# Re-cutting the loads at the start and at the end of a one-core cached-attention block: x and c in seven pieces for five, the last V tile in two for three, w2 in four for five, and two warm-up products for three

## The chip, the core and the metric

The kernel runs on one core of a Trainium2 chip. The core has a matrix engine (TensorE, PE in the profile; its weight loads are PEld), a vector engine (VectorE, DVE), a scalar engine (ScalarE, ACT), GpSimd (POOL) and a sequencer that does nothing but issue transfers (SyncE, SP). Sixteen DMA engines move data between the device memory and the core's on-chip memory. The metric is the device time of one execution in microseconds (us). The kernel before takes 393.93 us, the median of three runs that lie between 393.89 and 394.06 us.

## What is computed

Eight decode rows of a transformer block with conditioning: `x` and `c` are 8 x 512, there are 32 query heads on 8 key/value heads of size 128, and only the last 2048 of 8192 cached positions count. All numbers are float32.

```python
mod = (silu(c) @ w_mod)                       # 512 x 3072, cut into sa, ca, ga, sb, cb, gb
h = layernorm(x) * (1 + ca) + sa
q = (h @ wq)                                  # 512 x 4096
p = softmax(q k^T / sqrt(128))                # k, v: the last 2048 cached positions
x = x + ga * ((p v) @ wo)                     # 4096 x 512
h = layernorm(x) * (1 + cb) + sb
x = x + gb * (relu(h @ w1 + b1)**2 @ w2 + b2) # w1: 512 x 1792, w2: 1792 x 512
```

The keys and values that count are 8 x 8 x 2048 x 128 floats each, 134 MB of the 165 MB that one execution reads.

## The kernel before

One call of `tile_adaln_cached_attention_mlp` writes every engine's instructions out in a fixed order. There is no loop left at run time.

**The big loads.** The on-chip home of the streamed data is one tile `home` with four slots of 4 MB, and a tile `small` of 2 MB. The list `loads` (line 144) names what is streamed, in order: the two parts of `w_mod` (`mod 0`, 4 MB, and `mod 1`, 2 MB), `wq` (8 MB, two slots in one transfer), then the 16 K tiles and 16 V tiles of 4 MB with pieces of `wo` between them, and at the end the last of `wo`, two halves of `w1`, and `w2`. `pump` (line 152) issues the next load whenever the slot that it needs is free; all of these transfers are issued by SP, in this order. A few loads are cut into pieces, so that a consumer can begin with the first piece: the last V tile by `cuts` on line 103 (a half and two quarters), `w2` by the list on line 136 (row groups 0 to 8, 8 to 10, 10 to 12, 12, 13).

**The small loads.** `x` and `c` come as one array `xc`, in four groups of eight rows (line 65). Each group is one transfer of 8 rows x 256 floats or two of 8 rows x 128 floats (line 67); they are issued by ACT. The first of them waits until DVE has cleared the tile `xc_in`. Late in the kernel ACT also issues the loads of `b1` and `b2` (lines 503 and 504).

**Counters.** The program keeps eight counters of landed transfers, named DMAHW0 to DMAHW7, and the loads take them in turn, those of ACT and those of SP in one sequence. Before, `mod 0` has DMAHW0, the five pieces of `xc` have 1 to 5, `mod 1` has 6, `wq` has 7, and the first K tile has 0 again. A load that gets a counter for a second time is issued only when the load that had it before has landed: this is a wait of the issuing engine, and what stands behind it on that engine waits too.

**Compute.** At the start, `c` goes through silu (line 201 and on) and PE multiplies it with `w_mod` (L278), a normalised `x` becomes `h`, and PE multiplies it with `wq` (L304). For every K tile DVE transposes (L190), PE forms scores (L359), DVE and ACT make the softmax, and PE weighs V (L446). At the end come the products with `wo` (L486), then `w1` (L611), then the 56 products with `w2` (L630), which run through the 14 row groups of `w2` in order, two last steps on DVE (L638, L639), and the transfer of the result (L640). Ahead of the `w2` products stand three products of a constant whose result nobody reads, `spin(3)` on line 627 (L566); they keep PE at work while DVE makes the operand `rT`.

Of the kernel before, what the change touches and what calls it, by code (L numbers as in the profile page):

```python
# [19 lines left out]
def tile_adaln_cached_attention_mlp(  # L20
# [16 lines left out]
    B, HKV, SK, DH = k_cache.shape  # L37
# [26 lines left out]
    nc.vector.memset(xc_in, 0.0)  # L64
    for q in range(D // P):
        b = slice(32 * q, 32 * q + B)
        for x, y in ((0, 2),) if q < 3 else ((0, 1), (1, 2)):
            nc.scalar.dma_start(xc_in[b, x:y], xc[b, x:y])

    ident = consts.tile([P, P], F32, name="ident")  # L70
# [8 lines left out]
    big = NJ * DH  # L79
# [9 lines left out]
    def size_of(key):  # L89
        return "small" if key[0] in ("wo", "w1") or key == ("mod", 1) else "big"  # L90

    def load(key):
        kind, i = key
        held[key] = free[size_of(key)].pop(0)
        if key == ("wq", 0):
            return
        t = slots[size_of(key)][held[key]]
        if kind in "KV":

            hk, c = divmod(i, 2)  # L100
            v = k_cache[4 * c : 4 * c + 4, hk] if kind == "K" else v_cache[c::2, hk]
            v = v[:, SK - W :, :].rearrange("u (p j) d -> p u (j d)", j=NJ)
            cuts = (0, big // 2, big * 3 // 4, big) if key == ("V", 2 * HKV - 1) else (0, big)
            for x, y in zip(cuts, cuts[1:]):
                nc.sync.dma_start(t[:, x:y], v[..., x:y])
            return

        def rows(o, v):
            n = v.shape[1] * v.shape[2]
            nc.sync.dma_start(t[:, o : o + n].rearrange("p (a n) -> p a n", n=v.shape[2]), v)  # L110

        w1v = w1.rearrange("(p kc) n -> p kc n", p=P)

        def wo_rows(j):

            r = 2 * REP * DH
            return wo[j * r : (j + 1) * r, :].rearrange("(h p i) n -> p h (i n)", p=P, i=4)

        if kind == "wo":
            rows(0, wo_rows(i))  # L120
        elif kind == "mod":

            v = w_mod.rearrange("(p kc) n -> p (kc n)", p=P)
            nc.sync.dma_start(t, v[:, big:] if i else v[:, :big])
        elif kind == "wq":

            o = base[held["wq", 0]]
            nc.sync.dma_start(home[:, o : o + 2 * big], wq.rearrange("(p k) n -> p (k n)", p=P))
        elif kind == "tail":
            rows(0, wo_rows(HKV // 2 - 1))  # L130
            rows(big // 2, w1v[:, 0:2])
        elif kind == "w1":
            rows(0, w1v[:, 2:4])
        else:
            v = w2.rearrange("(p c) n -> p c n", p=P)
            for lo, hi in ((0, 8), (8, 10), (10, 12), (12, 13), (13, 14)):
                rows(D * lo, v[:, lo:hi])

    def slot(key, n, o=0):
# [12 lines left out]
    def pump():  # L152
        while at[0] < len(loads) and free[size_of(loads[at[0]])]:
            load(loads[at[0]])
            at[0] += 1
# [53 lines left out]
    lo = consts.tile([P, 1], F32, name="lo")  # L209
    hi = consts.tile([P, 1], F32, name="hi")  # L210
# [299 lines left out]
    for s in range(N + PV_LAG + 1):  # L510
        g, i = divmod(s, C)
        q, h = divmod(s, 2)
# [50 lines left out]
    def spin(n):  # L563

        for _ in range(n):
            nc.tensor.matmul(spin_ps, ident, ident[:, None, :].to_broadcast([P, 4, P]), start=True, stop=True)  # L566
# [57 lines left out]

    py = ps_m.tile([P, 512], F32, name="m_ps", tag="m_ps")
    nc.tensor.matmul(py[:, :P], qsel.rearrange("p q b -> p (q b)"), b2_in, start=True, stop=False)
    spin(3)
    for f in range(FC):
        for q in range(NQ):
            nc.tensor.matmul(  # L630
# [6 lines left out]
    y = work.tile([P, P], F32, name="y", tag="one_y", bufs=1)  # L637
# [39 lines left out]
```

## Time and profile before

| | |
|---|---|
| time, median of 3 runs | 393.93 us |
| time of the profiled execution | 394.02 us |
| its span, first to last instruction | 392.2 us |
| mean granted clock of PE | 0.891 |
| read from device memory | 164.67 MB, 420 GB/s over the span |
| PE, DVE, ACT busy (share of the span) | 65%, 56%, 12% |
| instructions | 4670 |

The span begins with the first instruction and ends with the last; about 1.8 us of the time lie outside it. A row of the page's table of instruction groups reads: line, engine, operation, what it writes and reads, how often, then busy time, mean length, and the idle time of the engine just before these instructions with what ended it. "SPq" and "ACTq" are the two engines that issue transfers. A row on a transfer gives the time from its issue until all of it has landed.

### The profile page before, as it was taken

To read this page: it belongs to the slowest core of one execution; us is meant where nothing else is said; L and a number is where in the kernel's file an instruction comes from. 1 tells how busy PE (TensorE), PEld (TensorE's weight loads), DVE (VectorE), ACT (ScalarE), POOL (GpSimd) and SP (SyncE) were. 2 spreads that over 40 slices of the span, in tenths; PEclk is the share of its full clock that TensorE was granted. 3 is DMA by queue.
4 is the path that set the end of the run, shared out by engine and by line. 5 is a ranking of instruction groups with operands and counts; after the bars stand their busy time and mean duration, and the time that the engine had idled before them with its cause. 6 is when DMAs were issued, how large, how long until landed. Compare 5 with 4: busy or idle time off the path is not lost.

```text
span 392.2 us, 4670 instructions
## 1 busy us (share of the span) xinstructions
PE 255.1 (65%) x2006; PEld 77.7 (20%) x2006; DVE 219.7 (56%) x315; ACT 46.3 (12%) x89; POOL 1.3 (0%) x8
## 2 busy tenths in 40 slices
PE   0091958879228973797384837873774828896796
PEld 0030211112002321222021202221221202233324
DVE  1261099889056835783582817780775457855222
ACT  0120011221003100310031003000201003004010
POOL 0000000000000000000000000000000000000000
PEclk9997789989859996999699688999796969998989
DMA  8999999999999999999999999999999999999994
GB/s 329 430 435 439 440 435 431 428 430 401 453 428 428 426 431 428 430 431 446 423 426 435 428 433 435 430 424 431 407 450 431 426 431 436 432 423 408 427 424 178
DMA packets 7685, 165.04 MB, mean 421 GB/s; under 512 B 832, under 2 KB 1008, under 8 KB 1520
## 3 DMA queue, kind: packets, MB, share of 16 engines
q1 hardware_dynamic: 7568, 164.70, 98.3%
q8 instruction: 16, 0.26, 0.3%
q10 hardware_dynamic: 96, 0.04, 0.0%
q14 instruction: 5, 0.04, 0.0%
HBM read 164.67 MB, written 0.07 MB: 420 GB/s over the span
## 4 chain that ended last, share of the span: by engine, by line
DMA 62%; PE 19%; DVE 16%; issue 2%; SPq 0%; ACT 0%; DVEq 0%; ACTq 0%
DMA home<-in_A_k_cache_dram 46%; DVE kT L190 12%; DMA home<-in_A_wq_dram 9%; PE s_ps L359 8%; DMA home<-in_A_wo_dram 7%; PE m_ps L304 3%; PE o_ps L446 2%; PE q_ps L566 1%; DVE pT L425 1%; PE wo_ps L486 1%; PE m_ps L630 1%; PE m_ps L611 1%; PE p_ps L390 1%; DVE qbd L322 1%; DVE pr L418 1%
## 5 line engine op out<-in xcount | busy, mean ns | idle before, releaser
L190 DVE STREAM_TRANSPOSE kT<-home 128x1024 f32<-128x1024 f32 x128 | 151.1, 1219 | 87.0 <-DMA home<-in_A_k_cache_dram 83.6
L359 PE MATMUL s_ps<-kT,qst 128*32 128x512 f32 x512 | 129.4, 1076 | 21.5 <-DVE kT L190 20.6
L446 PE MATMUL o_ps<-home,pT 128*32 128x256 f32 x1024 | 69.8, 396 | 11.1 <-DVE pT L425 9.6
L446 PEld LDWEIGHTS o_ps<-home,pT 128*32 128x32 f32 x1024 | 33.5, 116 | 101.2 <-issue 60.5
L375 PE MATMUL m_ps<-ident,mx 128*1 128x128 f32 x16 | 4.3, 364 | 59.8 <-DVE mx L373 59.8
L359 PEld LDWEIGHTS s_ps<-kT,qst 128*32 128x32 f32 x512 | 14.5, 116 | 41.5 <-DVE kT L190 33.2
L425 DVE STREAM_TRANSPOSE pT<-pr 128x2048 f32<-128x2048 f32 x8 | 18.2, 2272 | 1.0 <-ACT pr L408 1.0
L408 ACT ACTIVATE pr<-pr,own 128x512 f32<-128x512 f32 x16 | 17.9, 1233 | 0.3
L402 ACT ACTIVATE pr<-p_ps,nm 128x512 f32<-128x512 f32 x8 | 5.5, 688 | 97.1 <-DVE nm L399 97.1
L369 ACT COPY ss<-s_ps 128x512 f32<-128x512 f32 x8 | 4.7, 587 | 100.6 <-issue 72.4
L347 ACT COPY qst<-q_ps 32x128 f32<-32x128 f32 x32 | 8.2, 257 | 70.2 <-PE q_ps L336 69.9
L304 PE MATMUL m_ps<-home,h1T 128*32 128x512 f32 x64 | 10.0, 793 | 8.7 <-DMA home<-in_A_wq_dram 8.7
L375 PEld LDWEIGHTS m_ps<-ident,mx 128*1 128x1 f32 x16 | 0.7, 81 | 65.0 <-DVE mx L373 65.0
L224 PE MATMUL m_ps<-xsum,sel 128*128 128x1 f32 x2 | 0.6, 362 | 19.8 <-DVE xsum L222 19.8
L322 DVE COPY qbd<-m_ps 32x128 f32<-32x128 f32 x8 | 3.0, 372 | 18.1 <-PE m_ps L319 18.0
L390 PE MATMUL p_ps<-ss,perm 128*128 128x512 f32 x16 | 11.3, 794 | 0.0
L399 DVE TENSOR_SCALAR nm<-m_ps 128x1 f32<-128x1 f32 x8 | 1.3, 158 | 15.8 <-PE m_ps L395 15.8
L418 DVE TENSOR_SCALAR pr<-pr,own 128x512 f32<-128x512 f32 x16 | 9.2, 657 | 0.8 <-ACT pr L402 0.8
L202 DVE TENSOR_SCALAR e_sb<-e_sb 128x128 f32<-128x128 f32 x1 | 0.2, 226 | 14.4 <-ACT e_sb L201 14.4
L429 PE MATMUL m_ps<-zs,tsel 128*128 128x8 f32 x16 | 2.9, 252 | 8.1 <-DVE zs L420 8.1
L463 DVE TENSOR_SCALAR o_sb<-o_ps,bit 128x128 f32<-128x128 f32 x16 | 4.9, 304 | 4.9 <-PE o_ps L446 4.9
L373 DVE TENSOR_REDUCE mx<-s_ps 128x1 f32<-128x512 f32 x8 | 5.3, 662 | 3.8 <-ACT ss L369 3.8
(124 smaller groups left out, 125.8 us busy)
## 6 DMA issues: line engine op xcount, KB each, us to landing
home<-in_A_k_cache_dram SPq DMA_DIRECT2D x16, 4096.0 KB, 27.0
home<-in_A_v_cache_dram SPq DMA_DIRECT2D x15, 4096.0 KB, 20.0
small<-in_A_wo_dram SPq DMA_DIRECT2D x3, 2048.0 KB, 31.1
home<-in_w_mod_dram SPq DMA_DIRECT2D x1, 4096.0 KB, 12.5
small<-in_w_mod_dram SPq DMA_DIRECT2D x1, 2048.0 KB, 16.9
home<-in_A_v_cache_dram SPq DMA_DIRECT2D x1, 2048.0 KB
home<-in_A_v_cache_dram SPq DMA_DIRECT2D x2, 1024.0 KB, 21.2
home<-in_A_wo_dram SPq DMA_DIRECT2D x1, 2048.0 KB, 25.5
```

What stands on the lines that cost most here:

```text
L190: nc.vector.transpose(KTS[q, j][:, rows], k[:, rows, 32 * j : 32 * j + 32])
L304: nc.tensor.matmul(pqs[r][32 * g : 32 * g + 32, :], hT[:, kc, :], w[:, 4 * r + g, :], start=(kc == 0), stop=(kc == NQ - 1),)
L322: nc.vector.tensor_copy(qbd[b, 4 * r : 4 * r + 4, j].rearrange("p g (b t) -> p t g b", t=REP), pT_[b].rearrange("p (t g b) -> p t g b", t= ...
L347: nc.scalar.copy(own[b, :, :, i, 0], pq[b, :P].rearrange("p (c m t) -> p c m t", c=2, t=REP))
L359: nc.tensor.matmul(s_ps[0][32 * g : 32 * g + 32, :], qst[hk % 2][:, P * (4 * c + u) + 32 * j :][:, :32], kT[:, u], start=(c == 0 and j == ...
L373: nc.vector.tensor_reduce(mx, s_ps[0], axis=AX.X, op=ALU.max)
L390: nc.tensor.matmul(sp, perm, SS_.pop(hk), start=True, stop=True)
L402: nc.scalar.activation(pr.rearrange("p j x -> p (j x)"), SS_.pop(hk), AF.Exp, bias=nm, scale=SCALE, accum_out=z)
L408: nc.scalar.mul(X_[hk][..., w], pr, own[:, w : w + 1])
L418: nc.vector.tensor_scalar(X_[hk][..., w], pr, own[:, w : w + 1], None, op0=ALU.mult)
L425: nc.vector.transpose(PT_[hk].rearrange("p e j r -> p j e r"), X_.pop(hk).rearrange("p j x w -> p j (x w)"))
L446: nc.tensor.matmul(O_[n][32 * g : 32 * g + 32, : 2 * DH], PT_[hk][:, e, j : j + 2].rearrange("p j r -> p (j r)"), vt[:, j : j + 2, :].rear ...
```

## The change

The change has four parts. The groups of eight rows of `xc` were three single transfers and one pair, and are now one single transfer and three pairs. The last V tile is loaded in two halves. Row groups 8 to 12 of `w2` are one transfer of 1 MB where they were two of half a megabyte. One of the three products of `spin` ahead of the `w2` products is gone.

```diff
@@ -64,7 +64,7 @@
     for q in range(D // P):
         b = slice(32 * q, 32 * q + B)
-        for x, y in ((0, 2),) if q < 3 else ((0, 1), (1, 2)):
+        for x, y in ((0, 2),) if q < 1 else ((0, 1), (1, 2)):
             nc.scalar.dma_start(xc_in[b, x:y], xc[b, x:y])
@@ -100,7 +100,7 @@
-            cuts = (0, big // 2, big * 3 // 4, big) if key == ("V", 2 * HKV - 1) else (0, big)
+            cuts = (0, big // 2, big) if key == ("V", 2 * HKV - 1) else (0, big)
             for x, y in zip(cuts, cuts[1:]):
                 nc.sync.dma_start(t[:, x:y], v[..., x:y])
@@ -133,7 +133,7 @@
             v = w2.rearrange("(p c) n -> p c n", p=P)
-            for lo, hi in ((0, 8), (8, 10), (10, 12), (12, 13), (13, 14)):
+            for lo, hi in ((0, 8), (8, 12), (12, 13), (13, 14)):
                 rows(D * lo, v[:, lo:hi])
@@ -624,7 +624,7 @@
-    spin(3)
+    spin(2)
     for f in range(FC):
```

The first place is the start of the program on SP. The rows are the first seven loads, each with the counters and engines that it waits for; `home` and `small` are the on-chip tiles, and the two loads from `w_mod` are `mod 0` and `mod 1`. Before:

```order
L124 DMA home<-in_w_mod_dram 128x8192
L124 DMA small<-in_w_mod_dram 128x4096
L128 DMA home<-in_A_wq_dram 128x16384
L105 DMA home<-in_A_k_cache_dram 128x1x8192 [waits DMAHW0_49]
L105 DMA home<-in_A_k_cache_dram 128x1x8192 [waits DMAHW1_49,PE_49]
L105 DMA home<-in_A_k_cache_dram 128x1x8192 [waits DMAHW7_49,DMAHW2_49,PE_49]
L105 DMA home<-in_A_v_cache_dram 128x1x8192 [waits DMAHW3_49,PE_49]
```

The same seven loads in the changed kernel:

```order
L124 DMA home<-in_w_mod_dram 128x8192
L124 DMA small<-in_w_mod_dram 128x4096 [waits DMAHW0_49]
L128 DMA home<-in_A_wq_dram 128x16384 [waits DMAHW1_49]
L105 DMA home<-in_A_k_cache_dram 128x1x8192 [waits DMAHW2_49]
L105 DMA home<-in_A_k_cache_dram 128x1x8192 [waits DMAHW3_49,PE_49]
L105 DMA home<-in_A_k_cache_dram 128x1x8192 [waits DMAHW4_49,DMAHW1_49,PE_49]
L105 DMA home<-in_A_v_cache_dram 128x1x8192 [waits DMAHW5_49,PE_49]
```

The seven pieces of `xc` now hold counters 1 to 7, so `mod 1` gets DMAHW0, the counter of `mod 0`, and has a wait that it did not have; `wq` gets DMAHW1, that of the first piece of `xc`, and also has a wait that it did not have.

The second place is the end of the program on SP, as a piece of the difference between the two (rows with - stand only before, with + only now); `in_B_w_dram` stands for `w1` and `w2`, and the loads of `w2` are the four or five last ones ahead of the result.

```order
 L105 DMA home<-in_A_v_cache_dram 128x1x8192 x2
-L105 DMA home<-in_A_v_cache_dram 128x1x4096
-L105 DMA home<-in_A_v_cache_dram 128x1x2048 x2
+L105 DMA home<-in_A_v_cache_dram 128x1x4096 x2
 L110 DMA home<-in_A_wo_dram 128x2x2048
 L110 DMA home<-in_B_w_dram 128x3584
 L110 DMA small<-in_B_w_dram 128x3584
 L110 DMA home<-in_B_w_dram 128x4096
-L110 DMA home<-in_B_w_dram 128x1024 x2
+L110 DMA home<-in_B_w_dram 128x2048
 L110 DMA home<-in_B_w_dram 128x512 x2
 L640 DMA out_dram<-y 128x128
```

Two loads fewer are issued there; the order of the others is the same, and no other engine's order differs but PE's, by the one constant product, and ACT's, by the pieces of `xc`.

## The prediction

> **What bounds the kernel now.** I read the page first. Its second part shows the share of the sixteen DMA engines' time in 40 slices, and its fourth part the chain of waits that ended last.
>
> ```profile
> span 392.2 us, 4670 instructions
> DMA  8999999999999999999999999999999999999994
> DMA 62%; PE 19%; DVE 16%; issue 2%; SPq 0%; ACT 0%; DVEq 0%; ACTq 0%
> ```
>
> The engines are at 9 tenths or more in all slices but the first and the last, and the chain is mostly waits for loads. The DMA view cut to the stretch from 2.4 to 385.2 us says how full that is (queue, packets, MB, share of sixteen engines' time):
>
> ```profile
> DMA packets 7268, 163.93 MB, mean 428 GB/s; under 512 B 779, under 2 KB 827, under 8 KB 1117
> q1 hardware_dynamic: 7152, 163.61, 99.8%
> ```
>
> The queue that SP fills keeps all sixteen engines busy for 99.8% of those 382.8 us. There is no idle time in which a lost moment could be made good: a hole in the queue is paid in full at the end, and time on the other engines counts only where it makes the queue run dry, or behind the last load.
>
> Next I read the timeline of the first 16 us, where the counters of the loads are first used again (start, length, engine, line):
>
> ```profile
> 0.73 0.39 SPq L124 DMA_DIRECT2D home<-in_w_mod_dram  x1
> 1.16 2.03 ACTq L68 DMA_DIRECT2D xc_in<-in_xc_dram  x5
> 1.18 0.42 SPq L124 DMA_DIRECT2D small<-in_w_mod_dram  x1
> 1.64 0.42 SPq L128 DMA_DIRECT2D home<-in_A_wq_dram  x1
> 13.29 0.63 SPq L105 DMA_DIRECT2D home<-in_A_k_cache_dram  x1
> 15.10 1.28 ACT L201 ACT_TABLE_LOAD   x1 [15.10 <-DMA xc_in<-in_xc_dram]
> ```
>
> SP puts 14 MB into the queue within 2.1 us: `mod 0`, `mod 1`, `wq`. Its fourth load goes at 13.29. The view of SP's waits says why (who waited for whom, total, times, longest):
>
> ```profile
> SPq L105 <- DMA home<-in_w_mod_dram: 11.2, 1, 11.2
> ```
>
> That is the counter DMAHW0: the first K tile waits until `mod 0` has landed. It costs nothing there, since `mod 1` and `wq` are queued behind `mod 0` meanwhile.
>
> **The pieces of xc.** Seven pieces take seven counters, so that `mod 1` inherits the counter of `mod 0`. SP will then issue `mod 1` where it now issues the first K tile, at about 13.3 us and not at 1.18; `wq` stands behind it on SP and goes at 13.7, the first K tile after that. The queue holds nothing but `mod 0` until then, so the engines run dry, and the queue starts anew. How long a start lasts is bounded by the page's rows on issues (KB, us from issue to landing):
>
> ```profile
> home<-in_w_mod_dram SPq DMA_DIRECT2D x1, 4096.0 KB, 12.5
> small<-in_w_mod_dram SPq DMA_DIRECT2D x1, 2048.0 KB, 16.9
> out_dram<-y SPq DMA_DIRECT2D x1, 64.0 KB, 1.6
> ```
>
> `mod 1` lands now at 1.18 + 16.9 = 18.1 us. `mod 0` met an empty queue: 4.19 MB at 428 GB/s are 9.8 of its 12.5 us, and 2.7 are start and landing. The result's transfer also meets an empty queue: 0.07 MB are 0.15 of its 1.6 us, and 1.45 are start and landing. The 2.1 MB of `mod 1` flow in 4.9 us. With the one, `mod 1` would land at 13.3 + 2.7 + 4.9 = 20.9 us, 2.8 later than now; with the other at 13.3 + 1.45 + 4.9 = 19.65, 1.55 later. The row of `mod 0` is the nearer one: the same tensor, direction, 128 rows and size of pieces but for a factor of two. I take 2.4 and not its whole 2.8, because its 2.7 us hold things that are not paid again: the pieces of `xc` that share the engines with it, and the sixteen engines' first pieces at the program's start. That they are not instantaneous shows the DMA view of the first 3 us, in 40 slices of 0.075 us:
>
> ```profile
> GB/s 0 0 0 0 0 0 0 0 0 0 0 0 0 0 0 0 0 0 0 0 0 0 0 1748 1748 1311 0 0 437 0 0 437 437 437 0 437 0 0 0 0
> ```
>
> The first piece starts in the 24th slice, 1.0 us after the issue at 0.73, and the last engine's first one at 2.7. Both ends stay in the range.
>
> The Trainium skill, page "DMA: Bandwidth & Descriptors", section "Anatomy of one DMA — SWDGE (gpsimd) path", gives a fixed cost of about 2.0 us per transfer, for transfers issued by GpSimd; worked out from that page the landing would be at 13.3 + 2.0 + 4.9 = 20.2 us and the sum an estimated 396.0. The two rows of this trace, both of SP's transfers, lie on either side of that figure (1.45 and 2.7).
>
> The change of `xc` has another side, on ACT. Its five issues take 2.03 us, so that seven take about 2.8, and silu waits for the last piece, now until 15.10. A later or earlier arrival is covered by this row of the page's costliest groups:
>
> ```profile
> L304 PE MATMUL m_ps<-home,h1T 128*32 128x512 f32 x64 | 10.0, 793 | 8.7 <-DMA home<-in_A_wq_dram 8.7
> ```
>
> PE waits 8.7 us for `wq` after all work on `c` and `x` is done, and 2.4 us more when `wq` comes later. Two more pieces would have to add over 8 us; the five together landed in 15. I cost this at nothing. The same cover holds for the loads that wait for PE's use of `mod 0`.
>
> **The last V tile.** Its third quarter now lands together with the fourth. The DMA view of 345.0 to 345.7 us has the fourth quarter's landing, and the timeline the work behind it:
>
> ```profile
> 345.12 0.54 SPq L105 DMA_DIRECT2D home<-in_A_v_cache_dram  x1
> home<-in_A_v_cache_dram SPq DMA_DIRECT2D x1, 1024.0 KB, 21.2
> ```
>
> ```profile
> 366.05 1.90 PE L446 MATMUL o_ps<-home,pT 128*32 128x256 f32 x32
> 370.05 0.19 DVE L475 TENSOR_TENSOR oT<-tr,rz 128x32 f32<-128x32 f32 x1
> 371.34 0.16 PEld L486 LDWEIGHTS wo_ps<-home,oT 128*32 128x32 f32 x8 [2.23 <-DMA home<-in_A_wo_dram]
> ```
>
> The quarter lands at 345.12 + 21.2 = 366.3. The last 32 passes on PE, the work of half a tile, take 1.90 us and now begin at 366.05; they would begin at 366.3 and end 0.25 later. The operand `oT` is then ready at 370.5, and the product with `wo` waits for its own load until 371.34. The slack of 1.1 us covers the 0.25: nothing.
>
> **w2 and the constant product.** The timeline of the end, and the DMA view of the last piece of `w2`:
>
> ```profile
> 366.41 0.33 SPq L110 DMA_DIRECT2D home<-in_B_w_dram  x1
> home<-in_B_w_dram SPq DMA_DIRECT2D x1, 256.0 KB, 22.2
> ```
>
> ```profile
> 382.88 2.84 PE L566 MATMUL q_ps<-ident 128*128 128x512 f32 x6
> 383.98 0.28 DVE L623 SCALAR_TENSOR_TENSOR pr<-relu 128x112 f32<-128x112 f32 x1
> 385.65 2.78 PEld L630 LDWEIGHTS m_ps<-home,pr 128*32 128x32 f32 x104 [0.76 <-issue]
> 388.63 0.16 PEld L630 LDWEIGHTS m_ps<-home,pr 128*32 128x32 f32 x8 [0.21 <-DMA home<-in_B_w_dram]
> 389.77 0.35 SPq L640 DMA_DIRECT2D out_dram<-y  x1
> ```
>
> Each product is two passes, so the three constant ones are six in 2.84 us, and one is 0.95. Without it the `w2` products begin at 384.7, still behind `rT` (384.26). But the last piece lands at 366.41 + 22.2 = 388.6, and the last eight passes wait for it already, 0.21 us. Starting earlier makes that wait longer and the end no earlier: nothing. The merged piece has two of 256 KB behind it, 0.52 MB or 1.2 us, so it lands at about 387.4; 40 of the 104 passes (2.78 us, 27 ns each) need it or follow it before the last piece, 1.1 us, and end at 388.5, ahead of 388.6. So the merge adds nothing either.
>
> Two loads fewer on SP's queue save what a load costs a full queue. Of the 382.8 us 0.2% is not that queue's work, 0.8 us over some 46 loads, so at most 0.02 each. I take 0.05 for both.
>
> **The sum.** Against the profiled execution's 394.02 us: 394.02 + 2.4 - 0.05 = 396.4. The median of the runs lies 0.09 below that execution; the forecast for the median is 396.3 us.
>
> **The rivals.** The first is on the other side: *no hole*. The wait on `mod 0`'s counter is met before the engines run dry. It decides at the point where the counter is full more than 1.0 us (the first-piece delay above) ahead of the engines' last piece of `mod 0`. Then only the tail's edits are left, each worth nothing or 0.05: 393.9 us, no change. Against it: the first K tile waited for this very counter and went at 13.29, beside 0.73 + 12.5 = 13.2 for the full landing; what speaks for it is only that no view shows when the pieces end. 6 in 100, with 2 more for a gain over 0.2% that I can't see.
>
> The second is *a dearer start*: seven pieces and two new waits make a second hole, `wq` coming too late behind `mod 1`. Its condition is that 2.1 MB (4.9 us) drain before `wq`, issued 0.45 us later, begins to flow, which would need a delay of over 4 us where the rows show 1.0 to 2.7. With a second start of 1.45 us the time is 397.8.
>
> The third is *a colder PE at the end*. PE stands still for up to 0.8 us ahead of the merged piece; if the granted clock fell, the 48 last passes would take longer. Rows by stage (after the busy times: granted clock, DMA share, GB/s):
>
> ```profile
> 38.00:48.00 10.00, 9.54 (x64) 2.64 (x64) 0.00 (x0) 0.34 (x1) 0.00 (x0) 0.68 1.03 441
> 386.00:387.00 1.00, 1.00 (x47) 1.00 (x42) 0.00 (x0) 0.00 (x0) 0.00 (x0) 1.00 0.53 211
> ```
>
> The clock was 0.68 behind an 8.7 us wait and 1.00 at the end. 48 passes at 27 ns are 1.3 us, at 0.68 they are 1.9; less the 0.1 of slack it is 0.5 more, 396.8. The Trainium skill, "TensorE: Matmul & The Clock Gate", Part 1, has the clock fall after an idle window of about 3.4 us; by that rule this rival does not come about, and the trace agrees as far as it goes. With the second it gets 9 in 100 beyond the range's upper end.
>
> **How the numbers follow.** A hole of about 2.4 us: 80 in 100 within the range. Its low end is the low row, 393.93 + 1.55 - 0.05 = 395.4, less 0.4 for `mod 0` landing sooner with nothing queued behind it: 395.0. The high end is 393.93 + 2.8 + 0.25, if the V tile's cover fails: 397.0. A smaller hole (394.7 to 395.0) has 3 in 100. A measurement of this kernel tells about 0.2%, 0.8 us, from no change. Slower: 80 + 9 + 3 = 92 in 100; within 0.2%: 6; faster: 2.
>
> **What the changed profile would show.** SP's rows would have `mod 1` at about 13.3 and `wq` at 13.7; the time from issue to landing of `mod 1` would be about 7 us instead of 16.9; the DMA slices of the first 20 us would have a hole near 13 to 15; the wait of ACT for `xc` would be no longer than now; everything from `wq` on would stand 2 to 3 us later; at the end PE would still wait for the last piece of `w2`, longer than 0.21 us. I am wrong if SP issues `mod 1` early, if the queue's later stretches turn out to have idle time that takes the shift in, or if a restart moves bytes much sooner than either row.

## The result, and the profile after

The changed kernel takes 396.63 us (median of six runs, 396.33 to 396.69), the kernel before 394.06 us on the same chips (six runs, 393.89 to 394.35). The ratio is 1.0063, with a 95% interval from 1.0052 to 1.0074: slower by 2.6 us. A few executions take 3 to 4 us longer than the others of their kernel (398.2 to 398.3 of the kernel before, 400.0 and 401.3 of the kernel with `xc` alone), so medians are given, and where such an execution is among them the interval of a ratio is wide. The profiled execution of the changed kernel took 396.65 us, its span is 394.9 us, 2.7 more than before.

The page of the changed kernel, parts 2 and 4 (shares of the DMA engines in 40 slices; the chain that ended last by engine):

```profile
span 394.9 us, 4667 instructions
DMA  8899999999999999999999999999999999999994
DMA 59%; DVE 22%; PE 14%; issue 4%; ACT 0%; SPq 0%; DVEq 0%; ACTq 0%
```

One slice has changed, the second, which reaches from 9.9 to 19.7 us: 8 tenths where 9 stood. The chain is still mostly waits for loads. The timeline of the start of the changed kernel:

```profile
0.73 0.39 SPq L124 DMA_DIRECT2D home<-in_w_mod_dram  x1
1.16 2.69 ACTq L68 DMA_DIRECT2D xc_in<-in_xc_dram  x7
13.21 0.33 SPq L124 DMA_DIRECT2D small<-in_w_mod_dram  x1
13.59 0.42 SPq L128 DMA_DIRECT2D home<-in_A_wq_dram  x1
14.06 0.64 SPq L105 DMA_DIRECT2D home<-in_A_k_cache_dram  x1
14.09 1.28 ACT L201 ACT_TABLE_LOAD   x1 [14.09 <-DMA xc_in<-in_xc_dram]
```

`mod 1` goes at 13.21 and not at 1.18. SP's waits in the changed kernel name what it waited for (who for whom, total, times, longest), and the page's rows on issues give the time to landing:

```profile
SPq L124 <- DMA home<-in_w_mod_dram: 12.1, 1, 12.1
```

```profile
home<-in_w_mod_dram SPq DMA_DIRECT2D x1, 4096.0 KB, 12.5
small<-in_w_mod_dram SPq DMA_DIRECT2D x1, 2048.0 KB, 7.6
```

The hole itself is seen in the DMA view from 12 to 16 us, 40 slices of 0.1 us, GB/s by the time at which a piece of a transfer starts. Before, and then after:

```profile
GB/s 0 164 164 169 671 835 497 328 164 0 655 983 492 328 0 164 502 998 671 328 0 164 328 655 819 655 0 0 164 983 819 492 164 0 164 819 983 328 328 0
```

```profile
GB/s 0 0 10 57 21 26 36 16 0 0 0 0 0 0 0 0 0 0 0 0 0 328 164 655 164 819 164 164 164 0 0 0 0 328 819 328 328 492 0 328
```

Before, a new piece starts in most tenths of a microsecond (32 of 40). After, only small amounts (the pieces of `xc`) start up to 12.8, then nothing until 14.1, 0.9 us after SP's issue. The last piece of `mod 0` itself starts between 11.4 and 11.5 (the DMA view from 10 to 14 us), so SP's queue starts nothing for 2.6 us; the pieces begun before still flow for a part of that. `mod 1` lands at 13.21 + 7.6 = 20.8 us where it landed at 18.1: 2.7 us later, and the span is 2.7 us longer. Nothing in between takes any of it in, as the DMA view of the changed kernel from 16 to 388 us shows for SP's queue:

```profile
q1 hardware_dynamic: 6776, 159.45, 100.0%
```

The end of the changed kernel, in its timeline:

```profile
374.12 0.16 PEld L486 LDWEIGHTS wo_ps<-home,oT 128*32 128x32 f32 x8 [0.88 <-DMA home<-in_A_wo_dram]
374.16 0.19 DVE L475 TENSOR_TENSOR oT<-tr,rz 128x32 f32<-128x32 f32 x1
384.77 1.98 PE L566 MATMUL q_ps<-ident 128*128 128x512 f32 x4
387.72 1.95 PE L630 MATMUL m_ps<-home,pr 128*32 128x128 f32 x64 [0.97 <-DMA home<-in_B_w_dram]
390.06 1.03 PEld L630 LDWEIGHTS m_ps<-home,pr 128*32 128x32 f32 x40 [0.66 <-DMA home<-in_B_w_dram]
391.36 0.16 PEld L630 LDWEIGHTS m_ps<-home,pr 128*32 128x32 f32 x8 [0.26 <-DMA home<-in_B_w_dram]
392.49 0.35 SPq L640 DMA_DIRECT2D out_dram<-y  x1
```

PE now waits for the first, the merged and the last piece of `w2` (0.97, 0.66 and 0.26 us), and goes on with the last one at 391.36, 2.73 us after the 388.63 of before. The end still hangs on the landing of the last bytes.

### The profile page after: what moved, and what is told of

The parts are those of the page before. It is cut to its first block, busy times and chain, and to the rows that moved or that the text cites. A ratio compares the mean times of both kernels' runs of the same rounds, so it can differ in the third digit from the quotient of the medians.

```text
span 394.9 us, 4667 instructions
## 1 busy us (share of the span) xinstructions
PE 255.0 (65%) x2004; PEld 78.1 (20%) x2004; DVE 219.7 (56%) x315; ACT 46.2 (12%) x89; POOL 1.3 (0%) x8
## 4 chain that ended last, share of the span: by engine, by line
DMA 59%; DVE 22%; PE 14%; issue 4%; ACT 0%; SPq 0%; DVEq 0%; ACTq 0%
DMA home<-in_A_k_cache_dram 37%; DVE kT L190 13%; DMA home<-in_A_wq_dram 7%; DMA home<-in_B_w_dram 6%; DMA home<-in_A_v_cache_dram 6%; PE s_ps L359 5%; DVE pT L425 4%; DMA home<-in_w_mod_dram 3%; PE p_ps L390 3%; PE m_ps L304 3%; DVE pr L418 2%; PE o_ps L446 2%; DVE mx L373 1%; DVE qbd L322 1%; PE m_ps L375 1%
## 5 line engine op out<-in xcount | busy, mean ns | idle before, releaser
L446 PE MATMUL o_ps<-home,pT 128*32 128x256 f32 x1024 | 71.1, 401 | 10.9 <-DVE pT L425 9.7
L446 PEld LDWEIGHTS o_ps<-home,pT 128*32 128x32 f32 x1024 | 34.4, 118 | 102.1 <-issue 59.8
L202 DVE TENSOR_SCALAR e_sb<-e_sb 128x128 f32<-128x128 f32 x1 | 0.2, 226 | 13.4 <-ACT e_sb L201 13.4
## 6 DMA issues: line engine op xcount, KB each, us to landing
home<-in_w_mod_dram SPq DMA_DIRECT2D x1, 4096.0 KB, 12.5
```

The lines of the kernel that those rows point to most:

```text
L446: nc.tensor.matmul(O_[n][32 * g : 32 * g + 32, : 2 * DH], PT_[hk][:, e, j : j + 2].rearrange("p j r -> p (j r)"), vt[:, j : j + 2, :].rear ...
```

## The experiments

The theory was that the whole loss is the one hole behind `mod 0`, made by the reuse of a counter, and that the tail's edits are free. The rivals were a share of the tail, and a cost of the small pieces as such. Each kernel is compared with the kernel before on the same chip.

| kernel | pieces of xc | time, us | before, us | ratio (95% interval) |
|---|---|---|---|---|
| tail alone | 5 | 394.0 | 394.02 | 0.9993 (0.9976 to 1.0010) |
| xc alone | 7 | 397.0 | 394.02 | 1.0088 (1.0055 to 1.0121) |
| six pieces | 6 | 393.95 | 394.02 | 0.9985 (0.9961 to 1.0009) |
| eight pieces | 8 | 394.03 | 394.02 | 0.9993 (0.9977 to 1.0010) |
| ten pieces | 10 | 396.76 | 394.1 | 1.0067 (1.0055 to 1.0080) |
| w_mod swapped | 7 | 396.47 | 394.1 | 1.0060 (1.0047 to 1.0074) |
| w2 in two loads | 5 | 395.23 | 394.1 | 1.0018 (0.9986 to 1.0049) |
| V tile in one load | 5 | 394.04 | 394.1 | 0.9999 (0.9990 to 1.0007) |

**The change cut in two.** First the changed kernel with only the edit of `xc` undone:

```diff
-        for x, y in ((0, 2),) if q < 1 else ((0, 1), (1, 2)):
+        for x, y in ((0, 2),) if q < 3 else ((0, 1), (1, 2)):
```

> The changed kernel with xc in five pieces again; the V tile in two, w2 in four, two constant products stay. Theory (the whole loss is the hole that mod 1 leaves by waiting for mod 0's counter): SP issues mod 1 at 1.2 us again, and the time is that of the kernel before, 394.0 us, within 0.3. Rival (part of the loss is from the tail: the V tile's merged half, the merged w2 piece or PE's clock): 394.5 or more.

Measured: 394.0 us. Then the reverse, the kernel before with only that edit made:

```diff
-        for x, y in ((0, 2),) if q < 3 else ((0, 1), (1, 2)):
+        for x, y in ((0, 2),) if q < 1 else ((0, 1), (1, 2)):
```

> The kernel before with xc in seven pieces and nothing else. Theory: all of the loss, 396.6 us, with mod 1 issued at about 13.2. Rival (the tail has a share): between 394.2 and 396.3.

Measured: 397.0 us. The loss is in the edit of `xc`. The tail by itself costs at most 0.4 us by the interval of its ratio, and nothing by its profile, where the result's transfer is issued at 389.69 against 389.77 before; its three edits were not tried one by one. That the kernel with `xc` alone lies 0.4 us above the changed one was expected by neither side. It isn't in the queue: SP issues `mod 1` later (13.38, not 13.21), but it lands after 7.4 us and not 7.6, at 20.8 in both, and the result's transfer is issued at 392.52 against 392.49. What makes the 0.4 stays open, and with the interval as wide as it is I read nothing from it.

**One piece more, one less.** If the loss came from the pieces as such, it would grow with their number. Eight pieces:

```diff
-        for x, y in ((0, 2),) if q < 1 else ((0, 1), (1, 2)):
+        for x, y in ((0, 2),) if q < 0 else ((0, 1), (1, 2)):
```

> The changed kernel with xc in eight pieces, one more. The counters move on by one: mod 1 then waits for the first piece of xc, wq for the second, and the eighth piece for mod 0. Theory: mod 1 goes at about 8 us and wq at about 10.5, while mod 0 still flows until 12.5, so the queue never runs dry and the time is back at 394.0 us, though there is a piece more. Rival (more small pieces slow the start, by sharing the engines or by their fixed cost): 396.6 or more, up to 397.9.

Measured: 394.03 us. The timeline of its start, and its DMA view from 12 to 16 us:

```profile
1.16 12.26 ACTq L68 DMA_DIRECT2D xc_in<-in_xc_dram  x8
7.95 0.33 SPq L124 DMA_DIRECT2D small<-in_w_mod_dram  x1
10.40 0.33 SPq L128 DMA_DIRECT2D home<-in_A_wq_dram  x1
12.89 0.64 SPq L105 DMA_DIRECT2D home<-in_A_k_cache_dram  x1
```

```profile
GB/s 5 497 0 343 1157 333 164 655 0 164 1311 328 164 333 333 169 1167 497 164 328 328 0 1311 492 164 328 174 164 1004 666 328 328 0 328 983 655 328 164 164 174
```

SP waits at three of its first four loads, 6.8, 2.1 and 2.1 us, and ACT's last piece waits too (the row of its issues ends at 13.42); but each load is in the queue before the one ahead has drained, so no hole opens. Six pieces:

```diff
-        for x, y in ((0, 2),) if q < 1 else ((0, 1), (1, 2)):
+        for x, y in ((0, 2),) if q < 2 else ((0, 1), (1, 2)):
```

> The changed kernel with xc in six pieces. mod 1 then has a counter of its own and goes at 1.2 us; the wait for mod 0 falls on wq, which goes at 13.2. Theory: mod 1 holds 4.9 us of transfer, more than the 2.7 that a start takes, so there is no hole and the time is 394.0 us. Rival one (any early wait of SP on mod 0 costs the same): 396.6. Rival two (each piece more costs its share): about 395.3.

Measured: 393.95 us, with this timeline:

```profile
1.18 0.42 SPq L124 DMA_DIRECT2D small<-in_w_mod_dram  x1
13.38 0.33 SPq L128 DMA_DIRECT2D home<-in_A_wq_dram  x1
```

The wait for `mod 0` is there, 11.8 us long, at the load behind. `mod 1` is in the queue meanwhile and its 4.9 us cover the start of `wq`. So a long wait of SP is not what costs; an empty queue is. Ten pieces, the check from the other side:

```diff
-        for x, y in ((0, 2),) if q < 1 else ((0, 1), (1, 2)):
-            nc.scalar.dma_start(xc_in[b, x:y], xc[b, x:y])
+        for x, y in ((0, 1), (1, 2)):
+            for l, r in ((0, P),) if q < 3 else ((0, H), (H, P)):
+                nc.scalar.dma_start(xc_in[b, x:y, l:r], xc[b, x:y, l:r])
```

> The changed kernel with xc in ten pieces (six of 128 columns, four of 64). mod 1 then waits for the third piece of xc, which landed at 13.0 in the changed kernel, a moment ahead of mod 0 at 13.2. Theory: the hole is back, SP issues mod 1 at about 13.0, and the time is 396.4 us, though eight pieces cost nothing. Rival (the eight-piece kernel was fast for another reason, such as the pieces being of one size): 394.0.

Measured: 396.76 us. Its timeline and its DMA view from 12 to 16 us:

```profile
12.93 0.33 SPq L125 DMA_DIRECT2D small<-in_w_mod_dram  x1
13.31 0.42 SPq L129 DMA_DIRECT2D home<-in_A_wq_dram  x1
```

```profile
GB/s 0 16 31 29 31 31 8 0 0 0 0 0 0 0 0 0 0 0 164 819 492 328 328 0 0 164 328 0 0 655 328 492 164 0 328 166 660 658 164 330
```

The hole is back. It is not that `c` and `x` come too late: PE still waits 6.1 us for `wq` behind its work on them. Five, six, seven, eight and ten pieces give 394.0, 393.95, 396.63 to 397.0, 394.03 and 396.76 us: neither the number nor the size of the pieces orders these times, but the moment at which `mod 1` is issued does (1.2, 1.2, 13.2 to 13.4, 7.95 and 12.9 us). In the changed kernel the last piece of `mod 0` starts by 11.5 us and has landed at 13.2: an issue well ahead of that is free, and one about then costs the hole.

**The price of a start.** The changed kernel with the two loads of `w_mod` in the other order:

```diff
-    loads = [("mod", 0), ("mod", 1), ("wq", 0), ("wq", 1), ("K", 0), ("K", 1)]
+    loads = [("mod", 1), ("mod", 0), ("wq", 0), ("wq", 1), ("K", 0), ("K", 1)]
```

> The changed kernel, seven pieces of xc, with the two loads of w_mod in the other order: mod 1 (2 MB) first, then mod 0 (4 MB), which now waits for mod 1's landing at about 8 us. Theory (a start of an empty queue has a fixed price, whatever stands before or behind it): mod 0 takes 12.5 us from issue to landing as it does at the program's start, and the time is 396.6 us again. Rival (the price is of the kernel's place or of the load's size): a half or a double of the hole, 395.3 or 399.

Measured: 396.47 us, and these rows of the timeline and of the issues:

```profile
0.73 0.39 SPq L124 DMA_DIRECT2D small<-in_w_mod_dram  x1
8.47 0.33 SPq L124 DMA_DIRECT2D home<-in_w_mod_dram  x1
```

```profile
home<-in_w_mod_dram SPq DMA_DIRECT2D x1, 4096.0 KB, 12.2
small<-in_w_mod_dram SPq DMA_DIRECT2D x1, 2048.0 KB, 7.7
```

By 428 GB/s the 4 MB take 9.8 us and the 2 MB 4.9, so start and landing cost 2.8 us here at the program's first start and 2.4 at the second. In the changed kernel they are 2.7 (12.5 - 9.8) and 2.7 (7.6 - 4.9), and with `xc` alone 2.8 (12.6 - 9.8) and 2.5 (7.4 - 4.9). Neither half of the hole nor twice the hole came about; first starts lie at 2.7 to 2.8 us, second ones at 2.4 to 2.7, read from one profile of each kernel.

**What covers the tail.** Two kernels with five pieces of `xc` push the tail's edits further, to see where they begin to cost. `w2` in two loads:

```diff
-            for lo, hi in ((0, 8), (8, 12), (12, 13), (13, 14)):
+            for lo, hi in ((0, 8), (8, 14)):
```

> Five pieces of xc, the other edits of the change, and w2 in two loads: row groups 0 to 8, then 8 to 14 in one piece. Theory (the tail's merge was free because 40 passes of PE fit between the merged piece and the last one): now all 48 passes follow the last byte, 1.3 us where eight passes (0.2 us) did, so 395.1 us. Rival (the end hangs on PE's own chain and not on the landing): 394.0.

Measured: 395.23 us. The interval of the ratio touches 1; the six executions lie between 395.13 and 395.67, and the profile's span is 393.4 us, 1.2 above before. The page's first line, and two rows of the timeline:

```profile
span 393.4 us, 4659 instructions
```

```profile
388.48 1.25 PEld L630 LDWEIGHTS m_ps<-home,pr 128*32 128x32 f32 x48 [1.86 <-DMA home<-in_B_w_dram]
390.07 0.29 DVE L638 TENSOR_TENSOR y<-m_ps,modC 128x128 f32<-128x128 f32 x1 [5.80 <-PE m_ps L630]
```

All 48 passes follow the landing and L638 starts 0.94 us after the 389.13 of before; the other 0.2 of the span lies behind the issue of the result's transfer. So the end is the landing plus the passes that need the last piece, and the change's own merge was free because two smaller pieces come behind it. The last V tile in one load:

```diff
-            cuts = (0, big // 2, big) if key == ("V", 2 * HKV - 1) else (0, big)
+            cuts = (0, big) if key == ("V", 2 * HKV - 1) else (0, big)
```

> Five pieces of xc, the other edits of the change, and the last V tile in one load. PE then has 64 passes, 3.8 us, behind the landing at 366.3, and the operand of the wo product is ready about 1.2 us after its own load. Theory (what is late there is late on PE, but PE has 0.9 us to spare since one constant product is gone): 394.0 to 394.4 us. Rival (the wo product sets the end): 395.2.

Measured: 394.04 us. In its timeline `oT` is ready at 372.23, 0.8 us after the product's load, and the end does not move:

```profile
371.45 0.16 PEld L486 LDWEIGHTS wo_ps<-home,oT 128*32 128x32 f32 x8 [0.33 <-DMA home<-in_A_wo_dram]
372.04 0.19 DVE L475 TENSOR_TENSOR oT<-tr,rz 128x32 f32<-128x32 f32 x1
373.44 0.43 DVE L569 COPY at_i<-wo_ps 128x256 f32<-128x256 f32 x1 [1.21 <-PE wo_ps L486]
384.78 1.95 PE L630 MATMUL m_ps<-home,pr 128*32 128x128 f32 x64 [0.94 <-DMA home<-in_B_w_dram]
388.43 0.16 PEld L630 LDWEIGHTS m_ps<-home,pr 128*32 128x32 f32 x8 [0.26 <-DMA home<-in_B_w_dram]
```

No experiment gave a kernel that is faster than the one before: what the cuts at the start and at the end can do is to leave the queue full, and it was full.

## Why the prediction was right

The forecast was 396.3 us and the measurement is 396.63. Of the difference, 0.13 is the kernel before, which took 394.06 beside the changed one and 393.93 in the forecast; the loss was put at 2.35 us and measured at 2.57. Step by step:

- *SP will issue `mod 1` at 13.3 and `wq` at 13.7.* Right: 13.21 and 13.59.
- *A start costs 2.4 us, between 1.55 and 2.8.* Right in kind and inside the range; this is the term of the sum that was a little too small. `mod 1` landed 2.7 us later and the span grew by 2.7. I had taken the row of `mod 0` (2.7, a shift of 2.8) and then taken 0.3 off, as an estimate, for things that would not be paid twice. In the changed kernel the second start cost 2.7 as the first did, so there nothing came off. In the two other kernels with seven pieces the second start cost 2.4 and 2.5 where the first cost 2.8, so the estimate was not wrong everywhere; what makes a second start cheaper in one profile than in another stays open. The low end of the range also took 0.4 off for `mod 0` landing sooner with nothing queued behind it: it took 12.5 us in both kernels.
- *A hole is paid in full at the end.* Right: SP's queue is at 100.0% from 16 to 388 us, and the shift at the last piece of `w2` (2.73) is that at the landing of `mod 1` (2.7).
- *The pieces of `xc` cost nothing themselves.* Right: ACT's seven issues took 2.69 us (2.8 expected), and the wait for the last piece ended at 14.09, earlier than the 15.10 of before, with the hole leaving the engines to the last pieces.
- *The last V tile is covered by 1.1 us of slack.* The conclusion was right; the working holds in some kernels and not in the changed one. I had `oT` 0.25 us later beside its load. Where the clock at the V passes was as before (1.00 from 362 to 368 us), that is nearly what came: with eight pieces L475 starts at 370.38, 0.33 after the 370.05 of before, and the product's load still comes last. In the changed kernel `oT` would by this working have been ready at 373.2, shifted by the 2.7 us, and it came at 374.35 (374.16 + 0.19), 0.2 after the product's load at 374.12: PE's passes with V ran at a clock of 0.50 and 0.63 from 362 to 368 us, where the corresponding stretches of before had 0.53 and 1.00. That these would run at the same clock was an unspoken condition. It cost nothing all the same, for a reason that I had not named: the `w2` products begin behind the landing of the first `w2` piece, with 0.97 us of waiting, so PE had time to spare. The V tile in one load shows that this cover is larger than the one that I counted on.
- *The merged `w2` piece lands 1.2 us ahead of the end and is free.* Right: PE's row for it is at 390.06, 387.4 before the shift of 2.7, and 387.4 was the estimate.
- *The constant product buys nothing.* Right: PE's wait for the last piece is 0.26 us where it was 0.21. That the wait grew by so little is because the start of the `w2` products is itself bound by a landing. No run takes this product out alone.
- *Two loads fewer save 0.05.* Not seen: the tail alone gives 394.0 beside 394.02, and a difference of 0.05 is less than these runs can tell.

Of the rivals, no hole and a dearer second start did not come about. The colder PE did not either: the clock is 1.00 from 384 to 392 us in the changed kernel. That the trace agrees with the rule named beside this rival holds only for the two stages shown there: in the same trace the clock was 0.68 from 371 to 374 us, behind rests of PE of at most 1.8 us (last section).

The Trainium skill, "DMA: Bandwidth & Descriptors", section "Anatomy of one DMA — SWDGE (gpsimd) path", has about 2.0 us for the fixed part of a transfer issued by GpSimd. For SP's loads into an empty queue the runs here show 2.4 to 2.8 us; an estimate by the page's figure would have come out at 396.0; the measured price decides.

## What to carry to other kernels

When a kernel keeps the transfer engines full, look at what gates the *issue* of each load, in the order of the queue: a wait of 12 us cost nothing where the loads still queued flowed for longer than a start takes (4.9 us against 2.4 to 2.8, with six pieces), and a wait that let the queue run empty cost a whole start, 2.7 us. What a load shorter than a start would cover was not tried. Completion counters that are handed out in turn couple loads that have nothing to do with each other; adding two tiny loads on one engine moved a wait onto a 2 MB load of another, and a third tiny load moved it away again. Count them whenever the number of transfers changes, at the start of the program above all, where few loads are in flight.

## What the runs showed of the hardware that was not expected

An empty queue's second start is about as dear as its first. Though the engines had been at work for 12 us, `mod 1` needed 2.7 us beyond its flow, as `mod 0` did at the program's start (2.7), and the first piece started 0.9 us after the issue (1.0 at the program's start). The lowest second start read here is 2.4.

The product with `wo` ran at two speeds, and the edit does not choose between them. The rows by stage (PE busy first, then PEld, DVE, ACT, POOL; granted clock, DMA share, GB/s), before:

```profile
362.00:365.00 3.00, 3.00 (x64) 1.66 (x60) 0.77 (x4) 0.00 (x0) 0.00 (x0) 1.00 1.00 413
368.00:371.00 3.00, 0.70 (x2) 0.30 (x2) 1.34 (x4) 0.00 (x0) 0.00 (x0) 1.00 1.04 438
371.00:374.00 3.00, 2.65 (x16) 0.50 (x16) 0.00 (x0) 0.00 (x0) 0.00 (x0) 0.68 1.02 435
```

The same stages in the kernel with the tail's edits alone, and then two of them in the eight-piece kernel, which has the same tail:

```profile
362.00:365.00 3.00, 3.00 (x38) 1.43 (x34) 0.45 (x2) 0.00 (x0) 0.00 (x0) 0.60 0.96 399
368.00:371.00 3.00, 1.97 (x26) 0.78 (x18) 0.83 (x3) 0.00 (x0) 0.00 (x0) 1.00 1.03 432
371.00:374.00 3.00, 2.12 (x20) 0.56 (x20) 0.94 (x3) 0.22 (x1) 0.00 (x0) 1.00 1.00 425
```

```profile
368.00:371.00 3.00, 0.99 (x10) 0.30 (x2) 1.35 (x4) 0.00 (x0) 0.00 (x0) 1.00 1.03 434
371.00:374.00 3.00, 2.69 (x16) 0.51 (x16) 0.00 (x0) 0.00 (x0) 0.00 (x0) 0.69 1.01 430
```

With the tail alone, PE works 1.97 of the 3 us ahead of the `wo` product and not 0.70, the clock stays at 1.00 and not 0.68, and the copy that follows (L569) starts at 373.32 and not at 374.37. But the eight-piece kernel, with the same V tile in two, is slow again. All ten profiles, with the stage of 3 us ahead of the product and the stage that holds it (from 368 and 371 us, and from 371 and 374 where the kernel is shifted):

| kernel | loads of the last V tile | PE busy ahead, us | clock at the product | its 16 passes (L486), us |
|---|---|---|---|---|
| before | 3 | 0.70 | 0.68 | 2.97 |
| w2 in two loads | 2 | 1.04 | 0.69 | 2.91 |
| eight pieces | 2 | 0.99 | 0.69 | 2.89 |
| six pieces | 2 | 1.05 | 1.00 | 1.92 |
| ten pieces | 2 | 0.76 | 1.00 | 1.92 |
| w_mod swapped | 2 | 1.53 | 1.00 | 1.92 |
| changed kernel | 2 | 1.76 | 1.00 | 1.92 |
| tail alone | 2 | 1.97 | 1.00 | 1.92 |
| xc alone | 3 | 1.56 | 1.00 | 1.92 |
| V tile in one load | 1 | 2.15 | 1.00 | 1.92 |

Three loads are once slow and once fast, and two loads are both as well. Nor does PE's share of work in the 3 us ahead decide by itself: 0.76 kept the clock and 1.04 did not. The fall costs one microsecond on a chain that in the kernels with the tail's edits ends in a wait for `w2`, so it does not reach the time. The Trainium skill, "TensorE: Matmul & The Clock Gate", Part 1, lets the clock fall after an idle window of about 3.4 us; in the kernel before it fell though PE had worked 0.70 us within the 3 us ahead and its longest rest was 1.8 us. What decides whether the clock falls there stays open.
